# The second layer's output product summed inside PSUM in one chained order, with second buffers for three x operands

## The chip, the cores and the metric

The kernel runs on one core of a Trainium2 chip. The metric is the device time of one execution in microseconds (us); the time before is the median of three runs, 1097.01 us (1096.8 to 1097.92). A core has five engines with a queue each: PE (TensorE, matmuls, with weight loads shown as PEld), DVE (VectorE), ACT (ScalarE), POOL (GpSimd) and SP (SyncE, which issues the DMAs here). A queue runs in order, and an instruction that waits for a semaphore holds up everything behind it. Matmul results land in PSUM, which has 8 banks of 512 fp32 columns in each partition.

## The reference

Attention over 4 batches of 576 tokens (8 heads of 64, a block mask), then two feed-forward layers over the 2304 tokens. The change is in the second layer:

```python
rms = np.sqrt(np.mean(x * x, axis=-1, keepdims=True) + 1e-06)
xn = x / rms * rms_g                      # 2304 x 512
g = xn @ w_gate                           # 512 x 1536
silu = g * (1.0 / (1.0 + np.exp(-g)))
val = xn @ w_val                          # 512 x 1536
return (silu * val @ w_out).astype(np.float32)   # 1536 x 512
```

## The kernel before, in words

Every fp32 product is made of three fp32r matmuls (high by high, high by low, low by high), so each operand is first *split*: ACT copies the rounded high part (line 109), DVE or POOL subtracts it to get the low part (line 119). In the second layer each product of 2 x 2 blocks is done with seven products in place of eight (Strassen's method in Winograd's form), named P1, P2, P5, P6, P7, P3, P4. The weight combinations for it are made earlier and lie in DRAM, the operand combinations are B11, B21, B22 (parts of the operand itself) and T1 to T4 (differences).

The second layer works on three blocks of 768 tokens, each as two halves of 384 columns. A block runs in two *groups* of three *pairs*; a pair is one 256-wide piece of the hidden width, with a gate stream and a value stream of seven products each (six matmuls of 384 columns per product, line 591). In these streams the sums of Winograd's form are made in PSUM: after P1 the bank is copied by ACT into another bank (`copied`, line 599), P6 then adds onto the copy, and so on. `gated` and `valued` (lines 650 to 680) apply the sigmoid and the product of gate and value, form T1 to T4 of the hidden operand and split the seven hidden operands of that pair.

After the three pairs of a group `output(group)` multiplies the hidden operands by w_out: 7 products x 3 pairs x 2 halves of the output width x 3 matmuls = 126 matmuls of 384 columns (lines 622 to 624). It goes in two chunks. The first holds P1, P5, P7 and P6 for all three pairs (pairs outside, products inside) in all eight PSUM banks, the second P3, P2 and P4 in six. When a chunk's last pair is done, each bank is added to an SBUF tile of its own, 14 tiles in all: in the first group of a block by ACT as a scaled copy (line 631), in the second by DVE as multiply and add (line 633). In the second group DVE and POOL then combine these 14 tiles in SBUF with seven additions for each half of the output width (lines 640 to 646), and `finish` (line 903) sends the eight result tiles to DRAM.

Between two blocks the seven x operands of the next block have to be split (`split_sums`, lines 790 to 797, 768 columns each). They have one buffer each, so a split waits until the running block has used that operand for the last time. `before_last` starts them after the last product of the block's last pair, two before `output` and two at each step of it. `normed` (lines 825 to 877) loads the block after the next one into the tile `xf` (line 829), normalises it and forms the sums T1 to T4 of x (line 786). The splits read `xf`, so this load waits for them.

The weights of all products come through a ring of 19 SBUF slots of 256 KB, loaded by SP in the fixed order `SEQ` (line 274). PSUM tiles are handed out by `mm()` (line 754) in turn, so that a new tile takes the bank of the eighth tile before it. The order of the instructions in each queue is not the program's: the framework plans it when the kernel is built, by priorities and its own estimate of when each instruction's inputs are there, and fixes it. That is why output matmuls stand among the last stream's in the trace.

Of the kernel before, what the change touches and what calls it, by code (L numbers as in the profile page):

```python
# [8 lines left out]
F32 = mybir.dt.float32  # L9
# [7 lines left out]
P = 128  # L17
# [32 lines left out]
def tile_attention_moe_moe(  # L50
# [196 lines left out]

    P1, P2, P5, P6, P7, P3, P4 = range(7)
    OPERAND = ("B11", "B21", "T1", "T2", "T3", "B22", "T4")
    O_CHUNKS = (((0, "B11"), (2, "T1"), (4, "T3"), (3, "T2")), ((5, "B22"), (1, "B21"), (6, "T4")))  # L250
    GROUPS = ((0, 1, 2), (3, 4, 5))

    def order_of(group):
# [9 lines left out]
    SEQ = []  # L263
    for group in GROUPS:
        SEQ += [(wc_dram[f][y], i) for (f, y), i in order_of(group)]
        SEQ += [(wco_dram[f], i) for chunk in O_CHUNKS for f in group for i, _ in chunk]
    fetched, used, slots = [0], [0], {}

    def fetch_to(n):
# [308 lines left out]
    def moe2(pools, x, parts, ps_mm, acc, finish, before_fc, before_last):  # L578
# [31 lines left out]
        def output(group):  # L610

            first, last = group[0] == 0, group[-1] == FC // 2 - 1
            for chunk in O_CHUNKS:
                banks = {(i, m): ps_mm() for i, _ in chunk for m in range(2)}
                for f in group:
                    for i, name in chunk:
                        w = slot()
                        hh, hl = h.pop((f, name))
                        for m in range(2):
                            ps = banks[i, m][:, 0:n]  # L620
                            wh, wl = w[:, m * P:(m + 1) * P], w[:, (2 + m) * P:(3 + m) * P]
                            pe.matmul(ps, wh, hh, start=(f == group[0]), stop=False)  # L622
                            pe.matmul(ps, wl, hh, start=False, stop=False)  # L623
                            pe.matmul(ps, wh, hl, start=False, stop=(f == group[-1]))  # L624
                    if f != group[-1]:
                        yield 2 * len(chunk) * mm3(n)
                for i, _ in chunk:
                    for m in range(2):
                        ps = banks[i, m][:, 0:n]
                        if first:  # L630
                            act.activation(acc[i, m], ps, AF.Copy, scale=UNSCALE)
                        else:
                            dve.scalar_tensor_tensor(acc[i, m], ps, UNSCALE, acc[i, m], ALU.mult, ALU.add)
                        if last and i in (5, 1, 6):
                            dm, half = {5: (0, 1), 1: (0, 0), 6: (1, 0)}[i]
                            finish(2 * dm + m, half * n, acc[i, m])
                if last and chunk is O_CHUNKS[0]:
# [10 lines left out]
                yield 2 * len(chunk) * mm3(n)  # L648

        def gated(pair, c, m, half):  # L650
            src = c[m, half]
# [28 lines left out]
                hidden(pair, "T4", t4, dve)  # L680

        for group in GROUPS:
            state = {}
            for z, i in order_of(group):
                (pair, wi), c = z, state.setdefault(z, {})
                use = gated if wi == 0 else valued
                args = (pair, c) if wi == 0 else (pair, c, state[pair, 0])
                if i == P1:
                    c[0, 0] = ps_mm()[:, 0:n]
                    product(c[0, 0], P1)  # L690
                    c["u2"] = copied(c[0, 0])
                elif i == P5:
                    ps = ps_mm()[:, 0:n]
                    product(ps, P5)
                    c["p5"] = sbuf("p5", 2)
# [24 lines left out]
            splits = iter(())  # L720
            if group[-1] == FC // 2 - 1:
                splits = before_last()
                for _ in range(2):
                    next(splits, None)
            for cost in output(group):
                yield cost
                next(splits, None)
                next(splits, None)
            for _ in splits:
                pass  # L730

# [43 lines left out]
    def sums_of(x):  # L775
# [11 lines left out]
            yield None  # L787
        yield b

    def split_sums(b, res):  # L790
# [91 lines left out]
    for at, (layer, t0, n_tok, parts) in enumerate(blocks):  # L882
        following = blocks[at + 1] if at + 1 < len(blocks) else None
        with_attention = at + 1 < NB
        if layer == 1 and blocks[at - 1][0] == 0:
            first_layer.close()
            hp = ctx.enter_context(tc.tile_pool(name="hp2", bufs=TF))
            tp = ctx.enter_context(tc.tile_pool(name="tp2", bufs=1))
            accs = ctx.enter_context(tc.tile_pool(name="acc2", bufs=1))
        if layer == 0:  # L890
            acc = accs.tile([P, KC, BMAX[0]], F32, tag="acc", name="acc")
        else:
            acc = {
                (i, m): accs.tile([P, BMAX[1] // 2], F32, tag=f"acc{i}{m}", name=f"acc{i}")
                for i in range(NC) for m in range(2)
            }
        norm = normed(*following[1:]) if following and following[0] == 1 else iter(())
        got = {}
# [130 lines left out]
```

## Time and profile before

| | |
|---|---|
| median of 3 runs | 1097.01 us (1096.8 to 1097.92) |
| the profiled execution | 1098.34 us |
| its span, first to last instruction | 1095.9 us |
| PE busy | 1058.8 us, 97% |
| PEld / DVE / ACT / POOL busy | 85% / 67% / 55% / 43% |
| mean granted TensorE clock | 0.997 |
| second layer in the span | from about 676 us to the end |

A line of a timeline gives start, duration, engine, source line, operation, the tile written and the tiles read, shapes and count, and in brackets the idle time of the engine before it with what released it. A matmul's shown duration (0.34 us) is longer than its share of the engine, as they are pipelined: starts follow each other by 0.17 to 0.18 us. hB, lB, hT and lT are the high and low parts of the x operands B.. and T..; hh and hl those of the hidden operands.

### The profile page before, as it was taken

How to read it: one execution, taken by the hardware profiler on the slowest of the kernel's cores; microseconds unless marked ns; L12 is line 12 of the kernel's file. 1: busy time of each engine (PE TensorE's matmuls, PEld its weight loads, DVE VectorE, ACT ScalarE, POOL GpSimd, SP SyncE). 2: the span in 40 equal slices, each digit the busy share in tenths (PEclk: the TensorE clock that was granted, in tenths of full speed). 3: DMA queues.
4: the chain of work that ended last, by engine and by line, in shares of the span. 5: the costliest groups of instructions: out<-in, count | busy, mean ns of one | idle time of the engine just before them, and what ended most of it. 6: DMA issues, size and time to landing. Idle time of an engine off the chain costs nothing.

```text
span 1095.9 us, 16755 instructions
## 1 busy us (share of the span) xinstructions
PE 1058.8 (97%) x5576; PEld 933.4 (85%) x5576; DVE 736.7 (67%) x1332; ACT 597.4 (55%) x1314; POOL 469.6 (43%) x451
## 2 busy tenths in 40 slices
PE   6989999999999999999999999999989999999998
PEld 4667676789998788788887888999989999899998
DVE  5766687656677877645637593783797828967177
ACT  6967767546665667534424442754537445354451
POOL 3746676525456676446525542121151202512023
PEclk9999999999999999999999999999999999999999
DMA  6755967978987887779978978798779788697873
GB/s 169 222 146 210 287 232 264 324 260 270 313 287 272 298 310 278 306 274 373 371 288 317 370 286 303 266 294 254 233 251 324 240 262 248 208 308 241 263 246 115
DMA packets 127594, 295.39 MB, mean 270 GB/s; under 512 B 41107, under 2 KB 52883, under 8 KB 114966
## 3 DMA queue, kind: packets, MB, share of 16 engines
q1 hardware_dynamic: 127510, 294.33, 78.9%
q8 instruction: 45, 0.74, 0.3%
q14 instruction: 39, 0.32, 0.1%
HBM read 232.93 MB, written 61.36 MB: 269 GB/s over the span
## 4 chain that ended last, share of the span: by engine, by line
PE 69%; DMA 7%; DVE 6%; POOL 5%; ACT 4%; issue 3%; POOLq 0%; DVEq 0%; SPq 0%; ACTq 0%
PE mm L591 21%; PE mm L563 7%; PE mm L562 7%; PE mm L561 7%; PE mm L523 3%; PE mm L622 3%; PE s L359 3%; PE mm L624 3%; PE mm L623 3%; PE mm L524 3%; PE mm L525 3%; DMA st<-in_w_ab_dram 2%; PE t L398 2%; PE t L458 2%; DMA st<-in_w_o_dram 1%
## 5 line engine op out<-in xcount | busy, mean ns | idle before, releaser
L119 POOL TENSOR_TENSOR hl<-g,hh 128x384 fp32r<-128x384 f32 (+2 forms) x76 | 92.3, 1214 | 372.6 <-ACT hh L109 372.0
L561 PE MATMUL mm<-xh,ab 128*128 128x512 f32 (+1 forms) x480 | 183.3, 385 | 0.0
L562 PE MATMUL mm<-xl,ab 128*128 128x512 f32 (+1 forms) x480 | 182.2, 380 | 0.5 <-POOL xl L119 0.5
L563 PE MATMUL mm<-xh,ab 128*128 128x512 f32 (+1 forms) x480 | 180.4, 376 | 0.0
L591 PE MATMUL mm<-hT,w 128*128 128x384 f32 x576 | 167.9, 340 | 5.7 <-issue 5.3
L591 PE MATMUL mm<-hB,w 128*128 128x384 f32 x432 | 127.5, 340 | 0.0
L109 ACT ACTIVATE hh<-g 128x384 fp32r<-128x384 f32 (+2 forms) x114 | 63.7, 558 | 108.1 <-DVE g L569 73.5
L383 POOL TENSOR_SCALAR pp<-pp,st 128x64 f32<-128x64 f32 (+3 forms) x144 | 89.4, 634 | 77.2 <-DVE st L380 61.8
L591 PEld LDWEIGHTS mm<-hT,w 128*128 128x128 f32 x576 | 106.6, 188 | 7.1 <-issue 5.9
L562 PEld LDWEIGHTS mm<-xl,ab 128*128 128x128 f32 x480 | 90.5, 188 | 17.9 <-issue 2.6
L561 PEld LDWEIGHTS mm<-xh,ab 128*128 128x128 f32 x480 | 90.4, 189 | 17.9 <-issue 2.8
L563 PEld LDWEIGHTS mm<-xh,ab 128*128 128x128 f32 x480 | 90.4, 188 | 16.2 <-issue 1.9
L591 PE MATMUL mm<-lT,w 128*128 128x384 f32 x288 | 97.9, 340 | 0.0
L359 PE MATMUL s<-ks,qz 128*128 128x384 f32 (+4 forms) x284 | 93.4, 421 | 1.6 <-ACT pp L368 1.5
L523 PE MATMUL mm<-hh,o 128*128 128x512 f32 (+1 forms) x240 | 91.0, 382 | 3.6 <-DVE acc L532 2.9
L368 ACT ACTIVATE pp<-s,st 128x288 f32<-128x288 f32 (+8 forms) x142 | 70.9, 502 | 40.5 <-DVE st L362 30.9
L524 PE MATMUL mm<-hh,o 128*128 128x512 f32 (+1 forms) x240 | 90.7, 380 | 0.0
L149 DVE SCALAR_TENSOR_TENSOR st<-st 128x512 uint32<-128x512 uint32 x72 | 68.2, 950 | 31.1 <-ACT st L144 29.9
L525 PE MATMUL mm<-hl,o 128*128 128x512 f32 (+1 forms) x240 | 87.0, 378 | 0.0
L622 PE MATMUL mm<-hh,w 128*128 128x384 f32 x252 | 84.3, 338 | 2.2 <-DVE c L714 1.1
L623 PE MATMUL mm<-hh,w 128*128 128x384 f32 x252 | 84.8, 336 | 0.0
L624 PE MATMUL mm<-hl,w 128*128 128x384 f32 x252 | 82.1, 337 | 0.0
(137 smaller groups left out, 2454.1 us busy)
## 6 DMA issues: line engine op xcount, KB each, us to landing
w<-wc SPq DMA_DIRECT2D x252, 256.0 KB, 3.5
ab<-wab SPq DMA_DIRECT2D x48, 1024.0 KB, 7.3
w<-wco SPq DMA_DIRECT2D x126, 256.0 KB, 3.5
st<-in_w_ab_dram SPq DMA_DIRECT2D x48, 512.0 KB, 4.4
o<-wo SPq DMA_DIRECT2D x16, 1536.0 KB, 7.9
wc<-bg SPq DMA_DIRECT2D x12, 1792.0 KB, 8.4
wab<-ab SPq DMA_DIRECT2D x12, 1024.0 KB, 5.2
wco<-bg SPq DMA_DIRECT2D x6, 1792.0 KB, 7.0
```

The lines of the kernel that those rows point to most:

```text
L119: eng_lo.tensor_tensor(lo, src, hi.bitcast(F32), ALU.subtract)
L359: pe.matmul(ps[:, 0:z - a], qz[m % 2][:, b], ks[m][:, a:z], start=True, stop=True)
L523: pe.matmul(ps[:, 0:n], wh, hh, start=(y == 0), stop=False)
L524: pe.matmul(ps[:, 0:n], wl, hh, start=False, stop=False)
L525: pe.matmul(ps[:, 0:n], wh, hl, start=False, stop=(y == TF - 1))
L561: pe.matmul(ps[:, 0:n], wh[:, a:z], xhc, start=(c == 0), stop=False)
L562: pe.matmul(ps[:, 0:n], wh[:, a:z], xlc, start=False, stop=False)
L563: pe.matmul(ps[:, 0:n], wl[:, a:z], xhc, start=False, stop=(c == KC - 1))
L591: pe.matmul(ps, lhs, rhs[:, c, :], start=(start and c == 0 and y == 0), stop=(c == 1 and y == 2), skip_group_check=not start,)
L622: pe.matmul(ps, wh, hh, start=(f == group[0]), stop=False)
L623: pe.matmul(ps, wl, hh, start=False, stop=False)
L624: pe.matmul(ps, wh, hl, start=False, stop=(f == group[-1]))
```

## The change

`output` goes product by product in the order P1, P5, P6, P2, P7, P3, P4, all three pairs of the group inside each product, and makes the sums in PSUM as the streams do: ACT copies the two banks of P1 (u2), P6 adds onto the copy, which is copied to u3, P2 adds onto P1's own banks, P7 adds onto u3, which is copied to c10, P3 adds onto u2 and P4 onto c10. Each result part is added to one of eight SBUF tiles (P5 to two of them); the combining additions are gone. The weights' order in the ring follows. The splits of the next block's x begin earlier: B11 at P6 of the last pair's gate stream, T1 and T2 at P6 and P7 of its value stream, the other four one at each step of `output`. For that B11, T1 and T2 have a second set of buffers (`xe`), used for every second block. DVE's additions in place of 14 in the second group are 12, and ACT's copies are new there; the first group has 8 scaled copies and 6 copies on ACT and 4 additions on DVE in place of 14 scaled copies on ACT.

```diff
-    O_CHUNKS = (((0, "B11"), (2, "T1"), (4, "T3"), (3, "T2")), ((5, "B22"), (1, "B21"), (6, "T4")))
+    O_ORDER = (P1, P5, P6, P2, P7, P3, P4)
...
-        SEQ += [(wco_dram[f], i) for chunk in O_CHUNKS for f in group for i, _ in chunk]
+        SEQ += [(wco_dram[f], i) for i in O_ORDER for f in group]
...
+            def product_o(banks, i, start=True):
                 for f in group:
-                    for i, name in chunk:
-                        w = slot()
-                        hh, hl = h.pop((f, name))
+                    w = slot()
+                    hh, hl = h.pop((f, OPERAND[i]))
...
+            def add(dm, half, m, ps, new=False, done=True):
+                t = acc[dm, half, m]
+                if new:
+                    act.activation(t, ps, AF.Copy, scale=UNSCALE)
+                else:
+                    dve.scalar_tensor_tensor(t, ps, UNSCALE, t, ALU.mult, ALU.add)
+                if last and done:
+                    finish(2 * dm + m, half * n, t)
...
+            for i in O_ORDER:
+                if i == P1:
+                    c00 = fresh()
+                    product_o(c00, P1)
+                    u2 = [copied(ps) for ps in c00]
+                elif i == P5:
+                    p5 = fresh()
+                    product_o(p5, P5)
                     for m in range(2):
-                        p = {i: acc[i, m] for i in range(NC)}
-                        dve.tensor_tensor(p[3], p[3], p[0], ALU.add)
-                        pool.tensor_tensor(p[5], p[5], p[2], ALU.add)
-                        dve.tensor_tensor(p[4], p[4], p[3], ALU.add)
-                        pool.tensor_tensor(p[5], p[5], p[3], ALU.add)
-                        pool.tensor_tensor(p[1], p[1], p[0], ALU.add)
-                        dve.tensor_tensor(p[6], p[4], p[6], ALU.add)
-                        dve.tensor_tensor(p[2], p[2], p[4], ALU.add)
-                        finish(2 + m, n, p[2])
+                        add(1, 1, m, p5[m], new=first, done=False)
+                        add(0, 1, m, p5[m], new=first, done=False)
+                elif i == P6:
+                    product_o(u2, P6, start=False)
+                    u3 = [copied(ps) for ps in u2]
+                elif i == P2:
+                    product_o(c00, P2, start=False)
+                    for m in range(2):
+                        add(0, 0, m, c00[m], new=first)
+                elif i == P7:
+                    product_o(u3, P7, start=False)
+                    c10 = [copied(ps) for ps in u3]
+                    for m in range(2):
+                        add(1, 1, m, u3[m])
+                elif i == P3:
+                    product_o(u2, P3, start=False)
+                    for m in range(2):
+                        add(0, 1, m, u2[m])
+                else:
+                    product_o(c10, P4, start=False)
+                    for m in range(2):
+                        add(1, 0, m, c10[m], new=first)
+                yield 2 * len(group) * mm3(n)
...
                     before_fc((2 * pair + wi) * 2)
+                    if pair == FC // 2 - 1:
+                        if wi == 0:
+                            splits = before_last()
+                        next(splits, None)
                     product(c["u2"], P6, start=False)
...
                     before_fc((2 * pair + wi) * 2 + 1)
+                    if pair == FC // 2 - 1 and wi == 1:
+                        next(splits, None)
                     product(c["u3"], P7, start=False)
...
             for cost in output(group):
+                next(splits, None)
                 yield cost
-                next(splits, None)
-                next(splits, None)
...
-            ("B11", dve), ("T2", dve), ("B21", dve), ("T1", dve), ("T3", pool), ("B22", dve), ("T4", pool),
+            ("B11", dve), ("T1", dve), ("T2", dve), ("B21", dve), ("T3", pool), ("B22", dve), ("T4", pool),
         ):
-            res[name] = [rms["sb"].tile(list(b[name].shape), F32R, tag=k + name, name=k + name) for k in "hl"]
+            to = early[0] if early and name in EARLY else rms["sb"]
+            res[name] = [to.tile(list(b[name].shape), F32R, tag=k + name, name=k + name) for k in "hl"]
...
+        early[:] = [xe] if layer == 1 and (at - NB_FIRST) % 2 == 0 else []
```

## Rows read from the trace of the kernel before

**Rows 1.** The page, part 1: busy time, share of the span, instructions.
```profile
PE 1058.8 (97%) x5576; PEld 933.4 (85%) x5576; DVE 736.7 (67%) x1332; ACT 597.4 (55%) x1314; POOL 469.6 (43%) x451
```

**Rows 2.** Waits of PE, 670 to 1100 us: who, releaser, total, times, longest.
```profile
PE mm L591 <- issue: 5.3, 2, 2.8
PE mm L622 <- DVE c L714: 1.1, 1, 1.1
PE mm L622 <- DVE acc L633: 1.1, 2, 0.8
```

**Rows 3.** Timeline of PE at the two block boundaries.
```profile
810.25 0.44 PE L622 MATMUL mm<-hh,w 128*128 128x384 f32 x1 [0.26 <-DVE acc L633]
...
814.93 0.34 PE L591 MATMUL mm<-hB,w 128*128 128x384 f32 x1
...
818.68 0.46 PE L591 MATMUL mm<-hT,w 128*128 128x384 f32 x1 [2.53 <-issue]
...
822.47 0.34 PE L591 MATMUL mm<-hT,w 128*128 128x384 f32 x1
...
951.82 0.45 PE L622 MATMUL mm<-hh,w 128*128 128x384 f32 x1 [0.80 <-DVE acc L633]
...
959.76 0.41 PE L591 MATMUL mm<-hT,w 128*128 128x384 f32 x1 [2.79 <-issue]
```

**Rows 4.** Stretches after them: window, busy of five engines (count), clock, DMA.
```profile
820.00:824.00 4.00, 4.00 (x18) 3.74 (x17) 3.09 (x6) 3.63 (x7) 0.00 (x0) 0.71 1.02 363
...
956.00:960.00 4.00, 1.21 (x7) 0.92 (x6) 4.00 (x8) 0.47 (x1) 0.90 (x1) 1.00 0.19 56
```

**Rows 5.** Timeline of DVE: before a second group, then at the boundaries.
```profile
752.81 0.56 DVE L655 TENSOR_TENSOR asb<-mm,sig 128x384 f32<-128x384 f32 x1 [14.96 <-ACT sig L653]
...
792.92 0.56 DVE L709 TENSOR_TENSOR c<-p,mm 128x384 f32<-128x384 f32 x1 [2.45 <-ACT mm L599]
...
802.16 0.96 DVE L119 TENSOR_TENSOR lB<-xf,hB 128x768 fp32r<-128x768 f32 x1 [0.18 <-ACT hB L109]
...
811.04 2.17 DVE L119 TENSOR_TENSOR lB<-xf,hB 128x768 fp32r<-128x768 f32 x1
...
814.54 2.64 DVE L642 TENSOR_TENSOR acc<-acc,acc 128x384 f32<-128x384 f32 x2
...
818.03 0.55 DVE L633 SCALAR_TENSOR_TENSOR acc<-mm,acc 128x384 f32<-128x384 f32 x1
...
959.11 2.87 DVE L633 SCALAR_TENSOR_TENSOR acc<-mm,acc 128x384 f32<-128x384 f32 x6
```

**Rows 6.** Groups by line, 700 to 1100 us: count, busy, mean ns, idle before.
```profile
L599 ACT ACTIVATE mm<-mm 128x384 f32<-128x384 f32 x100 | 46.7, 474 | 43.9 <-PE mm L591 43.7
...
L633 DVE SCALAR_TENSOR_TENSOR acc<-mm,acc 128x384 f32<-128x384 f32 x42 | 21.0, 548 | 0.6 <-issue 0.6
...
L641 POOL TENSOR_TENSOR acc<-acc,acc 128x384 f32<-128x384 f32 x6 | 8.2, 1375 | 6.3 <-DVE acc L633 6.3
L642 DVE TENSOR_TENSOR acc<-acc,acc 128x384 f32<-128x384 f32 x6 | 8.0, 1365 | 0.0
...
L640 DVE TENSOR_TENSOR acc<-acc,acc 128x384 f32<-128x384 f32 x6 | 3.0, 548 | 0.0
```

**Rows 7.** Timeline of PE where block 0's second output begins.
```profile
789.24 0.34 PE L622 MATMUL mm<-hh,w 128*128 128x384 f32 x1
...
797.34 0.34 PE L622 MATMUL mm<-hh,w 128*128 128x384 f32 x1
```

**Rows 8.** Timeline of DVE there: low part of the last pair's T1.
```profile
797.71 1.37 DVE L119 TENSOR_TENSOR hl<-asb,hh 128x384 fp32r<-128x384 f32 x1
```

**Rows 9.** Timeline of ACT after block 0.
```profile
820.10 0.84 ACT L832 ACTIVATE sq<-xf 128x768 f32<-128x768 f32 x1 [13.56 <-DMA xf<-x_dram]
...
821.58 0.47 ACT L599 ACTIVATE mm<-mm 128x384 f32<-128x384 f32 x1
```

**Rows 10.** Timeline of DVE at the end: the last output's last six banks.
```profile
1089.32 3.10 DVE L633 SCALAR_TENSOR_TENSOR acc<-mm,acc 128x384 f32<-128x384 f32 x6 [0.58 <-issue]
```

More of the change, by code (lines that the diff above doesn't have):

```diff
@@ L612, in output @@
             first, last = group[0] == 0, group[-1] == FC // 2 - 1
-            for chunk in O_CHUNKS:
-                banks = {(i, m): ps_mm() for i, _ in chunk for m in range(2)}
+            u2, u3, c00, c10 = {}, {}, {}, {}
+            def product_o(banks, i, start=True):
                 for f in group:
-                    for i, name in chunk:
-                        w = slot()
-                        hh, hl = h.pop((f, name))
[L619 to L627, printed above, removed]
-                    for m in range(2):
[L629 to L637, printed above, removed]
-                    for m in range(2):
-                        p = {i: acc[i, m] for i in range(NC)}
-                        dve.tensor_tensor(p[3], p[3], p[0], ALU.add)
-                        pool.tensor_tensor(p[5], p[5], p[2], ALU.add)
-                        dve.tensor_tensor(p[4], p[4], p[3], ALU.add)
-                        pool.tensor_tensor(p[5], p[5], p[3], ALU.add)
-                        pool.tensor_tensor(p[1], p[1], p[0], ALU.add)
-                        dve.tensor_tensor(p[6], p[4], p[6], ALU.add)
-                        dve.tensor_tensor(p[2], p[2], p[4], ALU.add)
-                        finish(2 + m, n, p[2])
-                yield 2 * len(chunk) * mm3(n)
@@ new lines, in product_o @@
+                    w = slot()
+                    hh, hl = h.pop((f, OPERAND[i]))
+                    for m in range(2):
+                        wh, wl = w[:, m * P:(m + 1) * P], w[:, (2 + m) * P:(3 + m) * P]
+                        for y, (lhs, rhs) in enumerate(((wh, hh), (wl, hh), (wh, hl))):
+                            pe.matmul(
+                                banks[m], lhs, rhs, start=(start and f == group[0] and y == 0),
+                                stop=(f == group[-1] and y == 2), skip_group_check=not start,
+                            )
@@ new lines, in add, with fresh @@
+            def add(dm, half, m, ps, new=False, done=True):
[6 more added lines that the diff above has]
+                    finish(2 * dm + m, half * n, t)
+            def fresh():
+                return [ps_mm()[:, 0:n] for _ in range(2)]
+            for i in O_ORDER:
[6 more added lines that the diff above has]
+                    product_o(p5, P5)
+                    for m in range(2):
+                        add(1, 1, m, p5[m], new=first, done=False)
[21 more added lines that the diff above has]
+                yield 2 * len(group) * mm3(n)
@@ L682, in moe2 @@
         for group in GROUPS:
-            state = {}
+            state, splits = {}, iter(())
             for z, i in order_of(group):
@@ L719, in moe2 @@
                 yield 2 * mm3(n)
[L720 to L723, printed above, removed]
-                    next(splits, None)
             for cost in output(group):
+                next(splits, None)
                 yield cost
-                next(splits, None)
-                next(splits, None)
             for _ in splits:
@@ L788, in sums_of @@
         yield b
+    EARLY, early = ("B11", "T1", "T2"), []
     def split_sums(b, res):
         for name, el in (
-            ("B11", dve), ("T2", dve), ("B21", dve), ("T1", dve), ("T3", pool), ("B22", dve), ("T4", pool),
+            ("B11", dve), ("T1", dve), ("T2", dve), ("B21", dve), ("T3", pool), ("B22", dve), ("T4", pool),
         ):
-            res[name] = [rms["sb"].tile(list(b[name].shape), F32R, tag=k + name, name=k + name) for k in "hl"]
+            to = early[0] if early and name in EARLY else rms["sb"]
+            res[name] = [to.tile(list(b[name].shape), F32R, tag=k + name, name=k + name) for k in "hl"]
             split(*res[name], b[name], act, el, "hh")
@@ L893, in tile_attention_moe_moe @@
             acc = {
-                (i, m): accs.tile([P, BMAX[1] // 2], F32, tag=f"acc{i}{m}", name=f"acc{i}")
-                for i in range(NC) for m in range(2)
+                (dm, half, m): accs.tile([P, BMAX[1] // 2], F32, tag=f"acc{dm}{half}{m}", name="acc")
+                for dm in range(2) for half in range(2) for m in range(2)
             }
```

1 line of the change is left out of this document (added).

## Prediction

> **What bounds the kernel now.** I read the page's first part first: PE is busy 97% of the span, no other engine over 85% [rows 1]. So a change that adds and removes no matmul can only win where PE stands still, and it can lose wherever it makes PE stand still. The next view is PE's waits over the second layer [rows 2]: 5.3 us in two waits before line 591, 1.1 us in two before line 622 for DVE's accumulation, 1.1 us in one for line 714. The reader is to see that this is all there is worth naming in more than 400 us, and that "issue" in the largest row only says that the profile found no releaser. The timeline tells where they are [rows 3]: both long ones stand at the two block boundaries, with a short one some 8 us before each.
>
> What ends the long ones is read from DVE's timeline [rows 5]. At the first boundary the next block's P1 starts at 814.93 and its six matmuls run; PE goes on at 818.68 with P5 (hT, operand T1). DVE's first accumulation out of the second chunk runs from 818.03 to 818.58, 0.1 us before that. Six banks are held by the second chunk, two more by P1 and its copy, so P5's tile is the bank that this accumulation frees. At the second boundary the six accumulations start at 959.11 and PE goes on at 959.76. In both places DVE has no idle time before: it comes through the splits and then line 642, two of which take 2.64 us, and lines 640, 645, 646, all ahead of the accumulations in its queue. PE waits for a bank; DVE is late because of splits and combining additions.
>
> After the first gap the clock falls: the stretch 820 to 824 was granted 0.71 [rows 4], so part of it ran at 1.2 GHz. The twelve matmuls from 818.68 to 822.47 took 3.79 us; at the spacing of 0.177 us (six in the 1.06 us of a product) they would take 2.12. That is 1.67 us more. After the second gap the clock stayed at 1.00 [rows 4].
>
> **What the change does to each engine.** PE: 126 matmuls an output before and after; nothing. DVE in a second output: 14 accumulations of 0.548 us, six additions of 0.548 and two of 1.365 go [rows 6], 13.7 us; twelve accumulations, 6.6 us, come. POOL loses six additions of about 1.4 us a block [rows 6], some 8 us. ACT gets six copies of 0.474 us an output [rows 6], 2.8 us; in a first output its instructions stay 14. A first output gets four accumulations on DVE, 2.2 us; DVE was idle for 14.96 us there [rows 5], so they cost nothing, and if that cover went they would delay the next group's gate stream by 2.2 us at most, which P1 and P5 of that stream hide in part.
>
> **The boundaries.** Without the combining additions, and with B11, T1 and T2 split before the output starts, DVE has between the end of the last stream's work at about 802 us [rows 5] and P1 at 814.93 [rows 3] only twelve accumulations and two splits: 6.6 + 2 x 0.96 to 2 x 2.17 us, 8.5 to 10.9, against 13 us. So it keeps up. The banks are also handed out otherwise: the next block's P1 and its copy take u2's two banks, read after P3 with P4's 18 matmuls (3.1 us) still to run, and P5 takes a bank of the output's P5, free long before. I take the whole of the waits: 0.26 + 2.53 + 1.67 = 4.46 us at the first boundary, 0.80 + 2.79 = 3.59 at the second [rows 3], together 8.05. What is late next there is the copy of P1 on ACT (rival B).
>
> The 1.1 us for line 714 [rows 2] stands in block 1's first group, just after DVE has waited for the normalisation's DMA; the change does not take that wait away. I count 0, with 1.1 as the other end.
>
> **The moved splits.** Three low parts per boundary now run on DVE among the last pair's streams. Alone one takes 0.96 us, beside POOL's work 2.17 [rows 5]. In the last value stream DVE has gaps, the longest 2.45 us [rows 5], so of 2.9 to 6.5 us two thirds find room and 1 to 3 us may push DVE's work back; the bill comes in the next step, where PE could notice.
>
> The Trainium skill (SBUF — State Buffer, section Who interferes with whom) says that a VectorE instruction with two SBUF inputs contends with a GpSimd instruction that reads SBUF. This trace agrees, with 0.96 against 2.17 us. By it the three splits would cost their long price whenever POOL splits a hidden operand beside them, and also the remaining ones would come nearer to the short one, since POOL's additions are gone. It moves no term of the sum, only the upper end of rival C.
>
> **The new order inside the output.** The copies hang on ACT: P1's two banks are copied while P5 runs, P6's while P2 runs, P7's while P3 runs. Each cover is 18 matmuls, 3.1 us, against 2 x 0.474 us. This leaves 2 us for anything that ACT has in hand (a high part of a split takes under 1 us), so I take 0; below 0 it cannot go, as PE has no wait there now. c10 takes c00's banks, which DVE frees after P2; P7 lies between, so 3.1 us cover again.
>
> The operands come in another order of need. Before, T1 of the last pair was wanted after 54 output matmuls, now after 30 (P1's 18 and P5's first 12). In block 0's second output 28 were done when the last stream ended at 797.34 (11 from 789.24 on [rows 7], 17 later), so the 31st would stand at 797.7; DVE finished T1's low part at 797.71 + 1.37 = 799.08 [rows 8]. That is 1.4 us late in strict order. But PE's queue is not in strict order: output matmuls were planned in front of the last stream's [rows 7], and P6's first twelve (2.1 us) need only the first pairs and u2. They cover 1.4 us if planned ahead of the late one. The bounds are 0 and 1.4 us in each of six outputs, 8.4 us, plus the pushed splits; by the row that it is nearest to (output matmuls used as filler) I take 1.0 us over all.
>
> **The end.** The last six accumulations ran from 1089.32 to 1092.42 [rows 10], each bank's as it became ready; now two follow the last product. The last one can't start earlier than the last matmul's end, before or after. I take 0, between -0.6 us (the output DMAs no longer queue on SP) and 0.
>
> **Sum.** Against the profiled execution, 1098.34 us with a span of 1095.9 and 2.4 us around it: -8.05 + 0 + 1.0 + 0 = -7.05, 1091.3 us. The profiled execution stood 1.33 us above the median of the runs, 1097.01; the same step from the median gives 1089.96, so **1090.0 us**. With the ends of the small terms (-1.1, -0.6, -1.0) it is 1087.3; with 3 us of late operands 1092.
>
> **Rivals.**
> *B: half the boundary gain.* ACT's queue holds the load wait of the normalisation: it sat idle 13.56 us for `xf` and only then came to the copy that the next block's P6 needs, at 821.58 [rows 9]. If that square is again planned ahead of P1's copy, P6 waits even with free banks. P6 could start after P1 and P5, 2.1 us after 814.93, so near 817.1, and P2 can't replace it, since it adds onto the bank being copied. The copy ended at 822.05; P6 would be 5 us late, less what of the next stream's P1 can step in (1.06 us), so about 4 us: 1094. Against it: `xf` is loaded when its last split is done, the remaining splits end some 5 us earlier, and so the load lands before the boundary. Only the first boundary has this.
>
> *C: slower, by late hidden operands.* If the plan puts P5's last pair right behind its first two, PE stands at all six outputs for T1. It pays 6 x 1.4 = 8.4 us, and another 1 to 3 us at each of the two boundaries' outputs for pushed splits: 10.4 to 14.4 us against 8.05. That is 1097.0 + 2.4 to 6.4, so about 1100. It decides from 1.4 us an output on, that is when the filler is not used. For it speaks that T1's low part took 1.37 us beside POOL [rows 8], which a plan may not know; against it that PE had no such wait in the long streams, where copies and operands follow each other just as closely [rows 2].
>
> *D: the chain costs the clock.* A stretch like that after 818.68 costs 1.67 us. If the waits for copies broke up all six outputs so far that each lost the clock once, that were 10 us, and the time 1097.0 - 8.05 + 10 = 1099. The Trainium skill (TensorE: Matmul & The Clock Gate, section A second HAM failure mode: psum-queue depth-cycling) describes it: a matmul kernel cycling through PSUM in which TensorE idles briefly and often keeps losing and regaining its clock. Here the streams already chain through PSUM copies, and the mean granted clock is 0.997, so this trace does not bear the rule out.
>
> *E: the plan shifts.* With every instruction of the second layer planned anew, small waits elsewhere eat the gain: about 1097.
>
> **How the numbers follow.** Forecast 0.62, B 0.15, C 0.12, D 0.03, E 0.08. A measurement of this kernel tells 0.2%, 2.2 us, from no change, so faster begins at 1094.8. The forecast and most of B lie there (0.75), E, the upper edge of B and C's lower edge are the same (0.13), the rest of C and D slower (0.12). The range goes from 1086.8 (all small terms at their lower ends and 0.5 us for the runs) up to 1096.5, which takes in B and part of E and leaves C and D out. The likeliest case alone has 1087.3 to 1092.
>
> **What would show it.** Right: no PE wait over 0.5 us at the two boundaries; the clock at 1.00 after them; DVE idle for some us between the output's last accumulations and the next block; lines 640 to 646 gone from POOL. Wrong: PE waiting inside the output before its P5 or P6 for a hidden operand's low part (C), or at the boundary for an ACT copy with `xf` behind it (B); or both boundaries clean and the time unchanged, with many new short waits in PE's list (E).

## The result, and the profile after

The median after is 1086.24 us (1084.42 to 1089.1, 4 runs) against 1096.9 us before in the same rounds (1095.82 to 1097.92): ratio 0.9905, interval 0.9881 to 0.9929. The forecast was 1090.0 and the range 1086.8 to 1096.5, so the median lies 0.6 us below the range. The direction and the place were right, but the gain was 10.7 us where 7.05 were counted. The profiled execution after took 1089.1 us with a span of 1087.3.

Layer 1, whose PE instructions keep their order, ends anywhere from 676.3 to 683.8 us into the profiles of this study. So I compare the *second layer* inside each profile: from the start of layer 1's last matmul (line 525) to the end of DVE's last accumulation. The timeline of PE has the start for before,

```profile
679.00 0.40 PE L525 MATMUL mm<-hl,o 128*128 128x512 f32 x1
```

with the end in [rows 10], 1089.32 + 3.10. After, PE's timeline and then DVE's:

```profile
681.59 0.40 PE L525 MATMUL mm<-hl,o 128*128 128x512 f32 x1
```

```profile
1083.02 1.08 DVE L632 SCALAR_TENSOR_TENSOR acc<-mm,acc 128x384 f32<-128x384 f32 x2 [2.04 <-PE mm L622]
```

That is 413.4 us before and 1084.10 - 681.59 = 402.5 after: 10.9 us less, the whole of the result.

PE's busy time is what it was [rows 1]; DVE lost 21 us and POOL 25 (the page, part 1):

```profile
PE 1059.8 (97%) x5576; PEld 933.2 (86%) x5576; DVE 715.4 (66%) x1314; ACT 602.1 (55%) x1332; POOL 444.9 (41%) x433
```

PE's waits over the second layer after (670 to 1100 us: who, releaser, total, times, longest). All rows of [rows 2] are gone; the one that is left was there before too, with 0.9:

```profile
PE mm L871 <- ACT sh L109: 0.9, 1, 0.9
```

The same view of PE's weight loads, before and then after, shows more of it:

```profile
PEld mm L591 <- issue: 5.9, 2, 3.1
PEld mm L622 <- DVE acc L633: 1.7, 2, 1.1
PEld mm L622 <- DVE c L714: 1.4, 1, 1.4
PEld mm L846 <- ACT sh L109: 1.2, 1, 1.2
PEld mm L591 <- ACT mm L599: 0.7, 1, 0.7
...
PEld mm L591 <- DVE asb L655: 0.2, 1, 0.2
```

```profile
PEld mm L871 <- ACT sh L109: 1.2, 1, 1.2
PEld mm L591 <- ACT mm L599: 0.4, 1, 0.4
PEld mm L622 <- ACT mm L599: 0.3, 1, 0.3
PEld mm L591 <- DVE asb L677: 0.2, 1, 0.2
```

With the row left out (0.3 for line 633) their sums are 11.4 and 2.1 us. The first boundary after, in PE's timeline, where [rows 3] had the gap of 2.53 us: the next block's P1 starts between output matmuls, and nothing has a wait in brackets.

```profile
815.24 0.33 PE L622 MATMUL mm<-hl,w 128*128 128x384 f32 x1
815.41 0.34 PE L591 MATMUL mm<-hB,w 128*128 128x384 f32 x1
```

The stretch keeps the full clock, 25 matmuls in 4 us, against 18 at 0.71 behind the gap [rows 4] (window, busy of five engines with counts, clock, DMA):

```profile
814.00:818.00 4.00, 4.00 (x25) 4.00 (x24) 2.88 (x5) 2.31 (x4) 0.00 (x0) 1.00 1.01 344
```

At the second boundary the three windows from 946 to 958 are at 1.00 as well.

DVE's timeline around the first boundary, where [rows 5] had it busy to the end: the moved splits lie at 789.30, 790.17 and 794.07, the output's accumulations come as their banks are ready, and 4.68 us are idle.

```profile
789.30 0.95 DVE L119 TENSOR_TENSOR lB<-xf,hB 128x768 fp32r<-128x768 f32 x1
790.17 0.94 DVE L119 TENSOR_TENSOR lT<-T,hT 128x768 fp32r<-128x768 f32 x1
...
794.07 1.13 DVE L119 TENSOR_TENSOR lT<-T,hT 128x768 fp32r<-128x768 f32 x1 [0.87 <-ACT hT L109]
...
804.45 2.02 DVE L119 TENSOR_TENSOR lB<-xf,hB 128x768 fp32r<-128x768 f32 x1 [0.51 <-ACT hB L109]
806.40 2.87 DVE L632 SCALAR_TENSOR_TENSOR acc<-mm,acc 128x384 f32<-128x384 f32 x6
809.88 0.56 DVE L632 SCALAR_TENSOR_TENSOR acc<-mm,acc 128x384 f32<-128x384 f32 x1 [0.61 <-ACT mm L599]
815.12 0.96 DVE L860 TENSOR_TENSOR sq<-sq,y 128x768 f32<-128x768 f32 x1 [4.68 <-ACT y L859]
```

POOL's timeline beside it:

```profile
793.37 1.01 POOL L119 TENSOR_TENSOR hl<-g,hh 128x384 fp32r<-128x384 f32 x1 [6.86 <-ACT hh L109]
...
803.76 4.41 POOL L119 TENSOR_TENSOR lT<-T,hT 128x768 fp32r<-128x768 f32 x2 [2.99 <-ACT hT L109]
```

A low part takes 0.95 us while POOL stands idle, 1.13 with 0.3 us of POOL beside it and 2.02 beside POOL's T3 and T4. The Trainium skill (SBUF — State Buffer, section Who interferes with whom) has a VectorE instruction with two SBUF inputs contend with a GpSimd instruction that reads SBUF; the trace agrees. The moved splits paid the short price, 3.0 us in all of the 2.9 to 6.5 that were allowed for.

ACT's timeline there: the square that waits for `xf` stood at 820.10 [rows 9] and now stands at 813.50, and no PE wait follows (rival B did not come).

```profile
813.50 0.85 ACT L857 ACTIVATE sq<-xf 128x768 f32<-128x768 f32 x1 [3.66 <-DMA xf<-x_dram]
```

### The profile page after: what moved, and what is told of

It is laid out like the page before. It is cut to its first block, busy times and chain, and to the rows that moved or that the text cites. A ratio compares the mean times of both kernels' runs of the same rounds, so it can differ in the third digit from the quotient of the medians.

```text
span 1087.3 us, 16722 instructions
## 1 busy us (share of the span) xinstructions
PE 1059.8 (97%) x5576; PEld 933.2 (86%) x5576; DVE 715.4 (66%) x1314; ACT 602.1 (55%) x1332; POOL 444.9 (41%) x433
## 4 chain that ended last, share of the span: by engine, by line
PE 77%; DMA 5%; ACT 4%; DVE 3%; POOL 3%; issue 2%; POOLq 0%; DVEq 0%; SPq 0%; ACTq 0%
PE mm L591 23%; PE mm L622 12%; PE mm L563 8%; PE mm L561 8%; PE mm L562 8%; PE s L359 4%; PE mm L523 3%; PE mm L525 3%; PE mm L524 3%; DMA st<-in_w_o_dram 3%; PE t L458 2%; PE t L398 2%; POOL x L150 1%; PE t L423 1%; POOL pp L383 1%
## 5 line engine op out<-in xcount | busy, mean ns | idle before, releaser
L622 PE MATMUL mm<-hh,w 128*128 128x384 f32 x504 | 125.6, 337 | 0.0
L599 ACT ACTIVATE mm<-mm 128x384 f32<-128x384 f32 x144 | 66.8, 475 | 85.6 <-PE mm L591 47.3
L622 PEld LDWEIGHTS mm<-hh,w 128*128 128x128 f32 x504 | 90.9, 188 | 0.3 <-ACT mm L599 0.3
```

The source lines that it names most:

```text
L622: pe.matmul(banks[m], lhs, rhs, start=(start and f == group[0] and y == 0), stop=(f == group[-1] and y == 2), skip_group_check=not start,)
```

## The experiments

Times of the second layer are from one profile each, read as above; two profiles of the kernel after differ by 0.3 us, those of before and after by 10.9. Ratios are against the kernel before, timed on the same chip. All their intervals but those of the strict order and of the thirty additions overlap with the change's, so what differs by 1 to 2.5 us among the other rows rests on one profile each and on the waits in it, not on the medians.

| kernel | second layer, us | median, us | ratio, 95% interval |
|---|---|---|---|
| before | 413.4 | 1096.9 | |
| after | 402.5 | 1086.24 | 0.9905, 0.9881 to 0.9929 |
| after, once more | 402.3 | 1087.72 | 0.9898, 0.9877 to 0.9919 |
| PSUM sums alone | 404.9 | 1089.84 | 0.9922, 0.9903 to 0.9942 |
| early splits alone | 404.4 | 1087.61 | 0.9908, 0.9885 to 0.9931 |
| before, additions later | 404.8 | 1088.78 | 0.9915, 0.9893 to 0.9937 |
| no second buffers | 403.1 | 1086.94 | 0.9898, 0.9882 to 0.9915 |
| PSUM sums, square behind the copy | 402.6 | 1089.56 | 0.9917, 0.9892 to 0.9942 |
| products in strict order | 409.3 | 1093.19 | 0.9954, 0.9937 to 0.997 |
| 20 additions, unfixed | 402.9 | 1087.97 | 0.9903, 0.9876 to 0.993 |
| 20 additions, two sums behind | 402.5 | 1084.69 | 0.9889, 0.9862 to 0.9917 |
| 8 additions, two sums behind | 401.9 | 1086.12 | 0.9899, 0.988 to 0.9918 |
| 30 additions, eight sums behind | 421.4 | 1104.48 | 1.0063, 1.0042 to 1.0085 |

**The kernel after, timed again** (no edit).

> The changed kernel again, unedited, so that the parts below stand beside it on one chip. Both theories: 1086 us give or take 2, 10 to 11 us under the kernel before; in the second layer no PE wait over 1 us.

The gain holds: 402.3 us, ratio 0.9898. The forecast's 1090.0 is outside what either set of runs gives.

### What PE waited for: three ways to let DVE come in time

**The kernel before, with the combining additions behind the second chunk's accumulations.** In blocks that another follows, the same instructions, in another order on DVE and POOL:

```diff
-                if last and chunk is O_CHUNKS[0]:
+                if last and chunk is O_CHUNKS[late_sums[0]]:
...
                         finish(2 + m, n, p[2])
+                        if late_sums[0]:
+                            for i, dm, half in ((5, 0, 1), (1, 0, 0), (6, 1, 0)):
+                                finish(2 * dm + m, half * n, p[i])
...
+        late_sums[0] = 1 if following else 0
```

> The kernel before, with one edit: in the blocks that have a successor the combining additions stand in the program behind the second chunk's accumulations, not ahead of them; as many instructions on every engine. Theory: the banks come free in time, the boundary waits go, 1088 to 1091 us, unless the additions, now beside the next block's first stream, make DVE late there by up to 3 us. Rival (PE waited for something else than DVE's queue order, such as weights or ACT): the waits of 2.5 us stay, 1096 to 1098 us.

404.8 us: 8.6 of the 10.9 us came back with no instruction added or removed. So PE waited because DVE came late to the accumulations, and the order of the work on DVE and POOL makes it late. It is not the place in DVE's queue alone. Counted from layer 1's last matmul, the second chunk's first accumulation starts at 132.5 us in place of 139.0. One each of lines 642, 645 and 646 no longer stands ahead of it, but the five low parts ahead of it also got shorter, 6.2 us in place of 8.6, with POOL's additions no longer beside them. The two causes were not taken apart. PE's waits:

```profile
PE mm L591 <- ACT mm L599: 2.0, 2, 1.8
...
PE mm L622 <- DVE c L717: 0.3, 1, 0.3
```

The waits for the accumulation are gone, and a wait for ACT's copy has come up in their place: rival B, at 1.8 us.

**The PSUM sums alone**, with the splits where they were:

```diff
-                    if pair == FC // 2 - 1:
-                        if wi == 0:
-                            splits = before_last()
-                        next(splits, None)
...
+            if group[-1] == FC // 2 - 1:
+                splits = before_last()
+                for _ in range(2):
+                    next(splits, None)
             for cost in output(group):
-                next(splits, None)
                 yield cost
+                next(splits, None)
+                next(splits, None)
...
-        early[:] = [xe] if layer == 1 and (at - NB_FIRST) % 2 == 0 else []
+        early[:] = []
```

> The new output alone; the x splits begin where they began before and have no second buffers. Theory (PE waited because DVE came late to free a bank, and the combining additions are 6 us of DVE's queue and 8 us of POOL's just there): the boundary waits stay away, 1086 to 1089 us, at most 1 us of wait at each boundary. Rival (the moved splits bring the gain): both boundary waits of 2.5 us and more are back, 1093 us or more.

404.9 us, with a wait longer than the 1 us that was expected. The 2.4 us that it lacks are rival B again, in PE's waits and in ACT's timeline: ACT stands idle for 6.27 us until the square can run, and the copy that P6 needs comes at 821.27. The row names an output's DMA as the releaser; the next run's row, equally long after layer 1, names the load of `xf`.

```profile
PE mm L591 <- ACT mm L599: 2.3, 1, 2.3
```

```profile
817.91 0.85 ACT L856 ACTIVATE sq<-xf 128x768 f32<-128x768 f32 x1 [6.27 <-DMA out_dram<-acc]
...
821.27 0.47 ACT L599 ACTIVATE mm<-mm 128x384 f32<-128x384 f32 x1
```

**The same with the square behind the copy** on ACT:

```diff
-            act.activation(to, ps, AF.Copy)
+            gate["u2"] = act.activation(to, ps, AF.Copy)
...
-        behind(act.activation(sq, x[:, 0, :], AF.Square), "hh")
+        ins = act.activation(sq, x[:, 0, :], AF.Square)
+        behind(ins, "hh")
+        behind(ins, "u2")
```

> The new output with the x splits as before (as in the run with the sums alone), and one order on ACT: the normalisation's first square, which waits for the load of xf, may not stand ahead of the streams' copy in PSUM given out last before it. Theory: the 2.3 us that remained in the run with the sums alone were P1's copy queued behind that square; they go, the second layer takes 402 to 403 us in place of 404.9, and 1086 to 1088 us come without any early split or second buffer. Rival: the copy was late for its bank, and 2 us of wait stay.

402.6 us, what the whole change gives, without its early splits; the median of 1089.56 is above the 1086 to 1088 that were expected. PE's list has one row left:

```profile
PE mm L872 <- ACT sh L109: 0.9, 1, 0.9
```

But ACT still stood idle for the load with work of the normalisation ahead of the copy, now another of its squares (line 860):

```profile
820.48 0.85 ACT L860 ACTIVATE y<-xf 128x768 f32<-128x768 f32 x1 [6.22 <-DMA xf<-x_dram]
821.23 0.47 ACT L599 ACTIVATE mm<-mm 128x384 f32<-128x384 f32 x1
```

Counted from layer 1's last matmul the load lets ACT go on at 136.7 us in both runs. The copy follows at 140.0 with the sums alone, behind three instructions of the normalisation of which one waited 1.02 us for DVE, and at 137.4 here, behind one. So the 2.3 us were not the load's wait by itself but what ran between it and the copy.

Rival B is thus real where the splits end late. In the whole change the load of `xf` is issued 124.9 us after layer 1's last matmul, with the sums alone 128.8, and no wait for the copy is left.

**The early splits alone**, on the kernel before (only B11 with a second buffer, since the 14 tiles leave no room for the others):

```diff
                     before_fc((2 * pair + wi) * 2)
+                    if pair == FC // 2 - 1:
+                        if wi == 0:
+                            splits = before_last()
+                        next(splits, None)
...
+    EARLY, early = ("B11",), []
```

> The early x splits alone, with the old output, its 14 tiles and its combining additions; only B11 has a second buffer, as the room for three is not there beside 14 tiles (T1 and T2 are not used any more where their splits begin). Theory: three low parts (3 to 6 us of DVE) less stand ahead of the second chunk's accumulations, which were 2.7 and 3 us late, so the boundary waits shrink to under 1 us each: 1088 to 1091 us, though the combining additions are all there. Rival (the combining additions are needed for it, or the moved splits make the hidden operands late): 1094 us or more.

404.4 us, and waits under 1 us each, as expected. PE still waits twice for DVE, and in DVE's timeline the last combining addition still stands right ahead of the accumulations, only earlier:

```profile
PE mm L591 <- DVE acc L633: 1.4, 2, 0.8
```

```profile
811.75 0.54 DVE L646 TENSOR_TENSOR acc<-acc,acc 128x384 f32<-128x384 f32 x1
812.22 1.01 DVE L633 SCALAR_TENSOR_TENSOR acc<-mm,acc 128x384 f32<-128x384 f32 x2
```

Each part alone gives 8.5 to 9.0 us, both give 10.9: they are substitutes, not terms to be added.

**The whole change without the second buffers**, so that the splits start at P6 of the last value stream:

```diff
-                    if pair == FC // 2 - 1:
-                        if wi == 0:
-                            splits = before_last()
-                        next(splits, None)
+                    if pair == FC // 2 - 1 and wi == 1:
+                        splits = before_last()
+                        for _ in range(2):
+                            next(splits, None)
...
-        early[:] = [xe] if layer == 1 and (at - NB_FIRST) % 2 == 0 else []
+        early[:] = []
```

> The changed kernel without the second buffers: B11's split begins with T1's, at P6 of the last value stream, when B11 has been used for the last time. Theory: DVE has 5 us of idle time in the output after the change, so the buffers are worth nothing measurable: second layer within 1 us of the changed kernel's 402.4 us (last matmul of layer one to last accumulation), 1085 to 1088 us. Rival: splitting B11 that late makes hidden operands late, 2 us or more.

403.1 us, 0.6 more than after, and a ratio that can't be told from that of the change: the buffers themselves buy next to nothing.

### What the filler is worth (rival C)

**Products in strict order** in every output: no product but P1 and P5 starts before the last matmul of the one before it.

```diff
+                            if f == group[0] and y == 0 and i not in (P1, P5):
+                                behind(ins, ("end", 0))
+                                behind(ins, ("end", 1))
...
+                for m in range(2):
+                    gate["end", m] = ends[m]
```

> The changed kernel with one constraint on the plan: in the output, P6, P2, P7, P3 and P4 may not be issued before the product ahead of them has ended, so that nothing can fill a wait for P5's last pair. Theory of the prediction's rival C: PE stands at P5 for the last pair's T1, 0.9 to 1.4 us in most of the six outputs and again at P6 for T2, 4 to 9 us in all, 1090 to 1095 us; that the unedited plan has no such wait is then the filler's work. Rival: the operands are in time anyway and the order is worth under 1 us.

409.3 us, 6.8 more than after. PE's waits that are new, DVE's queue ahead of the longest of them, and the clock behind it (windows):

```profile
PE mm L623 <- DVE hl L119: 3.2, 2, 2.4
PE mm L591 <- ACT mm L599: 1.6, 1, 1.6
```

```profile
729.87 1.60 DVE L898 SCALAR_TENSOR_TENSOR xf<-xf,rms_g,y 128x768 f32<-128x768 f32 x1
731.40 0.95 DVE L814 TENSOR_TENSOR T<-xf 128x768 f32<-128x768 f32 x1
732.26 0.55 DVE L119 TENSOR_TENSOR hl<-asb,hh 128x384 fp32r<-128x384 f32 x1
```

```profile
735.00:739.00 4.00, 4.00 (x18) 4.00 (x17) 0.56 (x2) 1.25 (x4) 0.00 (x0) 0.69 0.62 181
```

The last pair's low part stands behind the normalisation's instructions on DVE, PE waits 2.40 us for it, and the clock then falls: 18 matmuls in 4 us in place of 25. Such waits stand at two of the six outputs, by the weight loads at three, which is fewer than was expected. The 1.6 us are of another kind: rival B's late copy at the first boundary, where the last low part of x now ends 131.0 us after layer 1's last matmul in place of 124.9. By the weight loads PE stood 4.2 us for low parts and 1.9 for that copy, 7.3 in all against 2.1 after; with an estimated 1.7 us for the clock (4 us at 0.88 from 731 on, then 4 us at the 0.69 above) that makes 6.9, against 6.8 measured. In the kernel after, the planned order of PE's instructions in its first output shows why PE does not wait there (positions in the plan ahead, buffer numbers kept: 7460 and 7461 are P5's banks, 7456 and 7458 P6's, 7430 P2's):

```
3267 L622 MATMUL mm_7461<-hh_7206,w_7219 128x384 x2
3268 L622 MATMUL mm_7461<-hl_7207,w_7219 128x384
3269 L622 MATMUL mm_7456<-hh_7005,w_7249 128x384 x2
...
3276 L622 MATMUL mm_7460<-hh_7398,w_7229 128x384 x2
...
3286 L622 MATMUL mm_7430<-hh_7241,w_7299 128x384 x2
...
3288 L622 MATMUL mm_7460<-hl_7399,w_7229 128x384
```

P6's first pairs go ahead of P5's last high part, and P2's first pairs ahead of its low part. That filler is worth the greater part of the 6.8 us, the 4.2 us of waits for low parts and the clock's 1.7.

### Does DVE's lateness still reach PE?

**Twenty additions more on DVE** in the second output of the first two blocks, behind P2's accumulations (11 us; their results are used by nothing):

```diff
+                    if last and more[0]:
+                        extra = rms["sb"].tile([P, BMAX[1]], F32R, tag="sh", name="extra")
+                        for x in range(20):
+                            m = x % 2
+                            dve.tensor_tensor(extra[:, m * n:m * n + n], acc[0, 0, m], acc[0, 0, m], ALU.add)
```

> The changed kernel with 20 more additions of 128x384 on DVE after P2's accumulations in the last output of the blocks that have a successor; their results are not used. Theory: DVE's backlog at the boundary is what PE waits for; 20 x 0.55 = 11 us against some 5 us of idle time makes 3 to 6 us of wait at each boundary come back, 1091 to 1097 us. Rival: DVE's work there is off the path, and the time stays within 1 us of the changed kernel's.

A miss: 402.9 us. The plan had spread the additions among and behind the accumulations, so this told nothing of the theory. **Twenty, and then eight, with P3's two accumulations fixed behind them** (`gate["extra"]` is the last addition):

```diff
+                    ins = dve.scalar_tensor_tensor(t, ps, UNSCALE, t, ALU.mult, ALU.add)
+                    if last and done and (dm, half) == (0, 1):
+                        behind(ins, "extra")
```

> The same 20 additions as in the run before (results not used), but now DVE may issue P3's accumulations only behind them; these free the bank that the next block's P1 takes. Theory, mended: not the amount of DVE's work but its place ahead of the accumulations decides. From P2's accumulations at about 807 us, 11 us of additions end at 818, against P1 at 815: 2 to 4 us of wait at each of the two boundaries, a second layer of 406 to 411 us in place of 402.4, 1090 to 1096 us. Rival (DVE's order there is no matter either): second layer within 1 us of 402.4.

> The same with 8 additions ahead of P3's accumulations in place of 20. Theory: 4.4 us end at some 812 us, before P1's time, and cost nothing: second layer within 1 us of 402.4. Rival: each us of DVE's work ahead of the accumulations costs its share, 1.5 us or more over the two boundaries.

With twenty a second miss, 402.5 us; with eight 401.9, as expected, but that says nothing once twenty cost nothing. With twenty, PE's timeline has the next block's P1 at 810.39, and DVE's has P3's accumulations at 819.07:

```profile
810.39 0.34 PE L591 MATMUL mm<-hB,w 128*128 128x384 f32 x1
```

```profile
816.25 2.90 DVE L663 TENSOR_TENSOR extra<-acc 128x384 fp32r<-128x384 f32 x6
819.07 1.02 DVE L632 SCALAR_TENSOR_TENSOR acc<-mm,acc 128x384 f32<-128x384 f32 x2
```

So P1 and its copy don't need u2's banks, against what the prediction said. **Thirty additions, with all eight accumulations after P5's fixed behind them** (the additions now read `acc[0, 1, m]`):

```diff
-                    if last and done and (dm, half) == (0, 1):
+                    if last and done and more[0]:
                         behind(ins, "extra")
```

> The kernel after, with 30 additions of 128x384 on DVE (some 14.6 us by the 0.49 us spacing of the runs before) put into the second output of blocks 0 and 1 behind the accumulations of P5, and now every later accumulation of that output (eight of the twelve) is fixed behind them; their results are used by nothing. Theory: DVE's lateness still reaches PE, once it holds enough banks. Until the 30 are through, u2's, u3's, P1's and c10's banks stay taken, which is all eight, so the next block's first tiles have none; DVE comes to the eight accumulations near 820, where the next block's P1 would start near 810. That makes a wait of 5 to 10 us for PE at each of the two boundaries, the second layer 412 to 423 us in place of 402.5, the median 1096 to 1107. Rival: the accumulations no longer stand in PE's way at all (as the runs with 20 and 8 additions ahead of P3's alone would also allow): 402 to 404 us.

421.4 us, ratio 1.0063. PE's waits, and DVE's timeline at the first boundary:

```profile
PE mm L591 <- DVE acc L632: 14.9, 2, 9.4
```

```profile
817.58 5.23 DVE L661 TENSOR_TENSOR extra<-acc 128x384 fp32r<-128x384 f32 x11
822.73 3.80 DVE L632 SCALAR_TENSOR_TENSOR acc<-mm,acc 128x384 f32<-128x384 f32 x8
```

PE's P1 went on at 823.80. The eight follow each other by 0.46 us, so the second of them had ended 0.06 us before. At the second boundary P1 had run and P5 (hT) waited; PE and then DVE:

```profile
964.36 0.69 PE L591 MATMUL mm<-hT,w 128*128 128x384 f32 x1 [5.45 <-DVE acc L632]
```

```profile
963.76 3.33 DVE L632 SCALAR_TENSOR_TENSOR acc<-mm,acc 128x384 f32<-128x384 f32 x7
```

Here PE went on 0.06 us after the first of them ended. In the plan the first two are P2's, and P1's tile at the first boundary and P5's at the second lie in P2's banks. So the path from DVE to PE is still there, but through P2's accumulations: it is not how many banks are held that decides but which, and the runs with twenty and eight additions held P3's. That is read from these two places and the plan; P2's two alone were not held in any run. Such a gap also costs the clock (windows behind the first):

```profile
823.80:826.00 2.20, 2.20 (x7) 2.20 (x8) 2.20 (x6) 0.00 (x0) 0.00 (x0) 0.50 0.86 304
826.00:829.00 3.00, 3.00 (x14) 3.00 (x13) 1.40 (x3) 0.97 (x2) 0.00 (x0) 0.67 0.98 313
```

It was granted 0.50, which is 1.2 GHz, in the 2.2 us behind the gap and 0.67 in the next 3, so the second layer lost 18.9 us for 14.9 us of waits.

## Why the prediction was right, and where it was not

**Right.** PE stood still at the boundaries because a bank came free late, and it came free late because splits and combining additions were queued ahead of the accumulations on DVE, where they also ran longer beside POOL: in the reordered kernel before, PE's waits for accumulations are gone. With the change DVE has idle time, PE has no wait at either boundary, the clock stays at 1.00 there, POOL has no lines 640 to 646, and the moved splits found room. Rival B was rightly described, but for the normalisation's work behind the load, which is what made the copy late with the sums alone, and rightly put against the forecast: it takes 2.3 and 1.8 us where the splits stay late, 1.6 in strict order, and nothing in the whole change. Rival D did not come: the outputs chain through copies and the stretches read kept their clock. E did not come either.

**Wrong: the size of three terms.** The sum was -8.05 + 1.0 + 0 + 0 = -7.05, measured -10.9.

- *Late operands, +1.0 us.* They cost 0. The filler that the prediction named covers all of them. When it is forbidden, late low parts take 4.2 us and 1.7 us of clock, so rival C's mechanism exists, at two outputs and at less than the 10.4 to 14.4 us that it was given.
- *The wait for line 714, counted 0.* It is gone, 1.4 us by the weight loads. The reason given for keeping it, that DVE would still wait for the normalisation's DMA just ahead, did not hold. DVE's timeline, before and then after:

```profile
858.35 1.95 DVE L867 SCALAR_TENSOR_TENSOR xf<-xf,rms_g,y 128x768 f32<-128x768 f32 x2 [2.85 <-DMA y<-row]
```

```profile
853.04 1.94 DVE L892 SCALAR_TENSOR_TENSOR xf<-xf,rms_g,y 128x768 f32<-128x768 f32 x2
```

The normalisation begins sooner: its first square runs 141.1 us after layer 1's last matmul before and 131.9 after. The two waits shrink together: with the reordered additions 1.73 us are left on DVE and 0.7 on the weight loads, with the PSUM sums alone 0.44 and none.

- *The boundary waits, read from PE's rows.* The gaps of [rows 3] add up to 6.38 us; the weight loads stood idle for 5.9 + 1.7 = 7.6 there. A matmul's shown end is 0.34 us after its start while the next can start after 0.17, so a gap read between shown end and next start is short by the difference of 0.17. The Trainium skill (Perfetto Trace Analysis, section Tensor Engine Instruction (MATMUL, LD_WEIGHTS)) says that the profiler estimates a matmul's end; these rows agree. Start to start, the gap at 818.68 is 2.7 us beyond the usual spacing, where the row says 2.53. The start behind a gap comes late too, 0.28 us after the one at 951.82 in place of 0.18; the weight loads have both.

By the weight loads the sum closes: 11.4 - 2.1 = 9.3 us, and 1.67 for the clock, are 11.0 against 10.9 measured. Beyond the three terms, 1.0 + 1.4 + 1.2, this holds some 0.3 us in short waits, together 3.9: the difference between -7.05 and -10.9.

**Wrong: the low end of the range.** 1087.3 had line 714, the late operands and the end of the layer at their lower ends, but no lower end for the boundary waits themselves, which the prediction took as read and which were 1.2 us longer. And 0.5 us for the runs was too little: four runs of the kernel after spread over 4.7 us. So the median fell out of the range at its low end.

**Wrong: which banks.** That the next block's P1 takes u2's banks did not hold in the run with twenty additions, and in the run with thirty P1 and P5 waited for P2's accumulations. The rule behind it, that a tile takes the bank of the eighth tile before it, is not what the plan does: in the kernel after, c10 lies in the banks of the output's P5 and not in c00's, and at the first boundary P1 takes the bank that P2's second accumulation frees and P5 the one that P7's first frees. That no wait came all the same is luck, as far as this reasoning goes: P2's accumulations had ended at 809.27, 6 us ahead of P1.

## What to carry to other kernels

Where the bounding engine waits for another engine's queue, look first at what stands ahead of the release in that queue: here moving it, on DVE and on POOL beside it, gave 8.6 of 10.9 us without a new algorithm, and parts that each relieve the same wait must not be added up. Size PE's gaps from its weight loads or from start to start, not from shown ends. And look for what comes up behind the wait that goes: here a copy queued behind a normalisation that waits for a load took 2 us, until less of that work stood ahead of it or the load came sooner.

## What the runs showed of the hardware

Matmuls of 384 columns at a full clock have two steady spacings. Before, a first output ran 98 of them from 730.86 to 747.84, 173.3 ns each; after, block 1's second output and the streams' matmuls planned among it ran 137 from 927.08 to 951.28, 176.6 ns each. PE's windows (window, busy with count, clock, DMA), before and then after; each count has one matmul more, which begins or ends at the edge:

```profile
730.86:747.84 16.98, 16.98 (x99) 1.00 0.87 274
```

```profile
927.08:951.28 24.20, 24.20 (x138) 1.00 0.88 278
```

No wait is shown in either. The kernel after has the shorter spacing too, 51 matmuls from 731.40 to 740.24 at 173.3 ns each, so it is not the change that sets it. The cause stays open; over these 137 it is 0.45 us.
